# Experts' stage of an attention + capacity-routed MoE kernel: issue order of four engines from a booked model, six-round searches and lists on full 128x128 matmuls, W2 fetched apart from W1

## The chip, the core and the metric

The kernel runs on one core of a Trainium2 chip. The metric is the device time of one execution in microseconds. TensorE (PE in the profile) does the matmuls, VectorE (DVE) and ScalarE (ACT) the element-wise work, GpSimd (POOL) issues the gathers and scatters by index, SyncE (SP) issues the plain DMAs. Each engine works through its own queue in order; a semaphore holds an instruction until its operands are there, and everything behind it on that engine then waits too.

## What is computed

Two layers. The first is attention over 8 batches, 8 heads, 576 positions, with a local mask for four heads and a strided mask for the others. Its output, 4608 tokens of width 512, goes through eight experts, each with a capacity of 576 tokens:

```python
logits = x @ w_gate                      # x: [4608, 512], E = 8 experts
for idx in argsort(-logits.flatten()):   # greedy, best pair first
    tok, e = idx // E, idx % E
    if assigned[tok] >= 0 or counts[e] >= 576: continue
    assigned[tok] = e; counts[e] += 1
for e in range(E):
    h = maximum(x[assigned == e] @ w1[e], 0)     # 512 -> 1024
    out[assigned == e] = h @ w2[e]               # 1024 -> 512
```

## The kernel before

The change leaves the attention and the first expert's routing search (`search0`, L869) alone. What it rewrites is the stage of the eight experts, which begins where that search ends.

The greedy assignment is done expert by expert. An expert is "closed" at the score at which its 576th token is taken. `search` (L916) finds that score for the expert that fills next, on all 4608 tokens, 128 x 36, in `R1` = 7 rounds that each try `J1` = 17 thresholds: DVE compares every token with every threshold (L925), nine matmuls count the hits for four token columns at a time (L941, 68 output rows), DVE masks and sums them (L944, L947), one matmul folds the four column groups (L950), DVE compares with the capacity (L957), one matmul adds up over thresholds (L960), and DVE forms the next thresholds (L963). `number` (L981) then yields the expert's number; `weights` (L1079) reads it into a register of SP and issues eight DMAs of 512 KB for W1 and W2 (L1088); `slots` (L993) numbers the expert's tokens with a prefix sum (matmuls at L1010); `indices` (L1038) turns the slots into a token list with 36 matmuls of 32 output columns (L1064) and two that pick (L1072). `tokens` (L1167) gathers the rows with indirect DMAs on POOL (L1173) and turns them with transposing DMAs on SP (L1176; the first two or three tiles of expert 0 by PE, L1161).

Every weight matrix is split in a high and a low half-precision part: four squares on ACT (L1103) give a scale (a matmul at L1111), and eight cuts follow, each a scaled copy on ACT (L1121) and a difference on DVE (L1122). The f32 landing places of W1 and W2 exist once each, the split parts twice.

`ffn` (L1270) is the expert itself. Its first half, `hidden` (L1251), is 192 matmuls of W1 against the tokens (L1260) in eight groups; ACT (L1267) and DVE (L1268) take each group out of PSUM. Its second half is 96 matmuls of 512 columns (L1308) and 24 that run in pairs on 64 rows (L1302); ACT scales the result (L1318) and POOL scatters it (L1319).

The main loop (L1346 to L1365) walks through `ffn` and keeps a clock of PE's matmuls. The chains of the side work (search, slots, indices, weights) are generators that say after each step how long they sleep: fixed times such as `T_COUNT` = 2950, `T_SUM` = 1350, `T_STEP` = 1225 ns in a round and `T_PREFIX`, `T_HOT`, `T_LOAD` further on. Between two matmuls every chain that is due is advanced. `manual_schedule(engines=MAN)` makes the order written that way binding for PE alone (for ACT too in expert 0); the order on DVE, ACT, SP and POOL is the tile scheduler's, steered by `urgent()` (L837), which lifts the priority of a block. The chain of the next expert, in `side` (L1223), may not number an expert before the expert two ahead of it has been emitted (L1229).

Of the kernel before, what the change touches and what calls it, by code (L numbers as in the profile page):

```python
# [37 lines left out]
J1, R1, GC = 17, 7, 4  # L38
J0, JL, R0, CUTS0 = 32, 16, 6, (16, 12, 8)
TP = 128  # L40
# [5 lines left out]
URGENT = 4000  # L46
T_FIRST, T_COUNT, T_SUM, T_STEP, T_PREFIX, T_NEXT, T_HOT, T_DUP, T_LOAD = 1100, 2950, 1350, 1225, 3900, 2300, 4200, 550, 8000
PACE1 = 0.55
H0 = 256
HURRY = (0, 1, 7)  # L50
MAN, MAN0, MANP = {mybir.EngineType.PE}, {mybir.EngineType.Activation}, (0,)
T_W20, T_STEP0 = 9000, 1000
X1 = 100
SCALE_AT, TURN_AT, TAKE_AT, SEARCH_AT, TURN_U, W_EARLY, WARM0, WARM1, TURNS, TURN_E = 7, 9, 9, 10, 0, 1, 6, 4, 3, 2
T_F, T_LOAD0, T_HOT1, T_W, T_SQ, T_SCALE, T_CUT, T_BULK0 = 3000, 1500, 6350, 4000, 1500, 1500, 1500, 600
CUT0 = 1
EDGE0, PEAKS, PEAKS_N = 18, (24, 29), (1, 3)
LATE_Q, STORE_Q = (2, 3), ()
V_BITS, W1_BITS, W2_BITS = 8, 7, 15


def _constants():
# [31 lines left out]
    c["fold"] = np.concatenate([q[:, None] // J1 == x[None, :] // E, q[:, None] % J1 == np.arange(J1)[None, :]],  # L94
# [25 lines left out]
    pick = np.zeros((128, 2, 2, NT), np.float16)  # L120
    for g in range(4):
        for h in range(SHI):
            for a in range(3):
                for u in range(2):
                    for t in range(NT):
                        pick[32 * g + 3 * h + a, u, a // 2, t] = h == min(2 * t + u, SHI - 1)
    c["pick"] = pick.reshape(128, 4 * NT)
    c["iota"] = np.broadcast_to(np.arange(SLO, dtype=np.float16)[None, :, None], (TP, SLO, NC)).reshape(TP, SLO * NC)
# [4 lines left out]
def band_stride_attention_then_capacity_moe(ctx, tc, qt, kl, ks, nl, ns, wg, w1, w2, cst, out, dbg=None):  # L133
# [18 lines left out]
    fold = const.tile([GC * J1, GC * E + J1], F16, name="fold")  # L152
# [3 lines left out]
    pick = const.tile([128, 2, 2 * NT], F16, name="pick")  # L156
    iota = const.tile([TP, SLO, NC], F16, name="iota")
# [4 lines left out]
    nc.vector.memset(ones_j, 1.0)  # L162

    def late_constants():
        for t, name in ((desc8h, "desc_h"), (fold, "fold"), (small, "small"), (tri, "tri"), (pick, "pick"), (iota, "iota")):
            split_of = {"iota": NC, "pick": 2 * NT}.get(name)
            nc.sync.dma_start(t, cst[name].rearrange("q (s c) -> q s c", c=split_of) if split_of else cst[name])
        nc.sync.dma_start(val[:, :2], cst["val"].rearrange("q (a c) -> q a c", a=2))
# [667 lines left out]
    HV = 32  # L836
    rvb = [r1.tile([TP, HV, NC], F16, name=f"rv{i}") for i in range(2)]  # L837
    for t in rvb:
        nc.gpsimd.memset(t[:, 3 * SHI:], 0.0)
# [5 lines left out]
    def urgent(ph=1):  # L845
        return tc.high_priority(offset=URGENT * (2 if ph == 0 else 1))

    def spread(ph, todo):
        for step, f in todo:
            if ph not in rush:  # L850
                yield step if ph else min(step, T_BULK0)
            f()

    def slowly(todo):
        for step, f in todo:
            yield min(step, T_STEP0) if step != T_W20 else step
            f()
# [56 lines left out]
    def pace(t):  # L914
        return t if len(closed) > 1 else t * PACE1

    def search(rm, ohc, more):
        cand, src, top = cand0, rm, None
        ohv = ohc.rearrange("p c e -> p (c e)")
        for rd in range(R1):  # L920
            last = rd == R1 - 1
            t = cand[:, :J1] if last else cand[:, 1:J1 + 1]
            with urgent():
                cm = rt.tile([TP, NC, J1], F16, name="cm")
                nc.vector.tensor_tensor(cm, src[:, :, None].to_broadcast([TP, NC, J1]),  # L925
                                        t[:, None, :].to_broadcast([TP, NC, J1]), op=OP.is_ge)
                cv = cm.rearrange("p c j -> p (c j)")
                n = 1 if rd == R1 - 2 else J1 + 1
                if not last:
                    pre = cand[:, 0:1]  # L930
                    if n > 1:
                        pre = rt.tile([128, n], F32, name="pre1")
                        nc.vector.tensor_scalar(pre, steps[:, rd + 1, :n], cand[:, 0:1], None, op0=OP.add)
                if rd == 0:
                    more()
            yield pace(T_COUNT) + (X1 if len(closed) == 1 else T_FIRST if rd == 0 else 0)
            with urgent():
                pr = ps_r.tile([128, 512], F32, name="pr_")
                pc, p2, pm = pr[:GC * J1, :GC * E], pr[:J1, 64:64 + E], pr[:, 128:128 + (E if last else 1)]
                for k in range(0, NC, GC):  # L940
                    nc.tensor.matmul(pc, cv[:, k * J1:(k + GC) * J1], ohv[:, k * E:(k + GC) * E], start=(k == 0),  # L941
                                     stop=(k == NC - GC))
                red = rt.tile([GC * J1, GC, E], F16, name="red")
                nc.vector.tensor_tensor(red.rearrange("p c e -> p (c e)"), pc, fold[:, :GC * E], op=OP.mult)  # L944
                r8 = rt.tile([GC * J1, E], F16, name="r8")
                with nc.allow_low_precision(reason="whole numbers up to 1152"):
                    nc.vector.tensor_reduce(r8, red.rearrange("p c e -> p e c"), axis=AX.X, op=OP.add)  # L947
            yield pace(T_SUM)
            with urgent():
                nc.tensor.matmul(p2, fold[:, GC * E:], r8, start=True, stop=True, skip_group_check=True)  # L950
                g = rt.tile([J1, E], F16, name="g1")
                ih = rt.tile([J1, 1], F16, name="ih1")
                if last:
                    nc.vector.tensor_scalar(g, p2, float(CAP), None, op0=OP.is_ge)
                else:
                    with nc.allow_low_precision(reason="zero or one"):
                        nc.vector.tensor_scalar(g, p2, float(CAP), 0.0, op0=OP.is_ge, op1=OP.max, accum_out=ih)  # L957
            yield pace(T_STEP)
            with urgent():
                nc.tensor.matmul(pm, ones_j[:J1], g if last else ih, start=True, stop=True, skip_group_check=True)  # L960
                if not last:
                    cand = rt.tile([128, n], F32, name=f"cand{n}")
                    nc.vector.scalar_tensor_tensor(cand, steps[:, rd, J1 + 1:].to_broadcast([128, n]), pm, pre,  # L963
                                                   op0=OP.mult, op1=OP.add)
                if rd == R1 - 2:
                    top, src = cand, rt.tile([TP, NC], F32, name="rml")
                    nc.vector.tensor_scalar(src, rm, top, None, op0=OP.subtract)
                    cand = steps[:, rd + 1, :J1 + 1]
        with urgent():
            return settle(pm, top, steps[:, R1 - 1, J1 + 1:])  # L970
# [20 lines left out]
    def slots(ph, rm, ohc, wmc, code, mv):  # L991
        sc = rt.tile([TP, 2, NC], F16, name="sc")
        scf = sc.rearrange("p a c -> p (a c)")  # L993
        with urgent(ph):
            if mv is not None:
                mine = rt.tile([TP, NC], F16, name="mine")
                nc.vector.tensor_scalar(mine, wmc, code, None, op0=OP.is_equal)
                df = rt.tile([TP, NC], F32, name="df")
                nc.vector.tensor_scalar(df, rm, mv, None, op0=OP.subtract)
                nc.vector.scalar_tensor_tensor(sc[:, 0], df, steps[:TP, R1 - 1, J1 + 1:], mine, op0=OP.is_ge, op1=OP.mult)  # L1000
                nc.vector.scalar_tensor_tensor(sc[:, 1], df, 0.0, mine, op0=OP.is_ge, op1=OP.mult)
                nc.vector.tensor_tensor(sc[:, 1], sc[:, 1], sc[:, 0], op=OP.subtract)
            else:
                nc.vector.tensor_scalar(sc[:, 0], rm, -0.5 * BIG, None, op0=OP.is_ge)
                nc.vector.memset(sc[:, 1], 0.0)
        yield T_PREFIX
        with urgent(ph):
            pp = ps_r.tile([128, 512], F32, name="pr_")
            for j in range(2):
                nc.tensor.matmul(pp[:TP, j * 2 * NC:(j + 1) * 2 * NC], tri[:, j * TP:(j + 1) * TP], scf,  # L1010
                                 start=(j == 0), stop=(j == 1), skip_group_check=True)
            off = rt.tile([TP, 2 * NC], F32, name="off")
            nc.vector.tensor_scalar(off, scf, -8192.0, 8192.0, op0=OP.mult, op1=OP.add)
# [65 lines left out]
    def weights(ph, ei):  # L1079
        e = nc.sync.value_load(ei[0:1, 0:1], min_val=0, max_val=E - 1)  # L1080
        res, todo = [], []
        for name, w, nch, width, bits in (("w1", w1, DC, FF, W1_BITS), ("w2", w2, FC, DM, W2_BITS)):
# [3 lines left out]
            def fetch_w(cs, wf=wf, src=src, n4=n4):  # L1086
                for c in cs:
                    nc.sync.dma_start(wf[:, c * n4:c * n4 + n4], src[:, c * n4:c * n4 + n4])  # L1088
# [343 lines left out]
```

## Time and profile before

| | us |
|---|---|
| median of 3 runs | 702.52 (701.30 to 702.54) |
| the profiled execution, its own time | 707.31 |
| its span, first to last instruction | 705.5 |
| PE busy, DVE busy, ACT busy in the span | 613.3, 459.1, 360.9 |
| experts' stage, first to last of its main matmuls | 245.2 to 695.8 |

The profiled execution is 4.8 us above the median. Busy time of PE is modelled and overlapping matmuls count once, so a stage is read from the starts of the matmuls and from what PE waited for, not from the busy share.

### The profile page before, as it was taken

What the parts mean: (1) busy time and instruction counts of PE and PEld (TensorE: products, weight loads), DVE (VectorE), ACT (ScalarE), POOL (GpSimd) and SP (SyncE); (2) the same over time, 40 slices, a digit from 0 to 9 for tenths busy, and PEclk for the clock granted to TensorE, in tenths of its full rate; (3) what the DMA queues carried; (4) which work ended last, traced back from release to release, by engine and by line L of the source; (5) the groups of instructions that cost most, each with busy time, mean ns of one, the idle gap of its engine ahead of it and who ended that gap; (6) DMA issues with size and microseconds to landing.
All of it is one profiled execution on the core that took longest, in us unless ns stands there. A gap on an engine that the chain in (4) does not pass through costs nothing.

```text
span 705.5 us, 18314 instructions
## 1 busy us (share of the span) xinstructions
PE 613.3 (87%) x7519; PEld 398.8 (57%) x7519; DVE 459.1 (65%) x1377; ACT 360.9 (51%) x551; POOL 150.4 (21%) x166
## 2 busy tenths in 40 slices
PE   7686889888944599999999979998999998799994
PEld 3565667666733375457457437646645745455741
DVE  6678888888657779775775755766667563652210
ACT  7376778787420554761751643374185274743210
POOL 2041433143330300410320240050041032202011
PEclk9789999999775599999999998999999999899998
DMA  9987786874130740950860790392194089531001
GB/s 233 285 235 209 226 234 197 243 204 146 37 101 2 227 103 20 302 120 1 294 148 1 276 165 1 108 278 56 44 291 107 2 291 268 189 82 53 1 24 45
DMA packets 75776, 103.15 MB, mean 146 GB/s; under 512 B 43060, under 2 KB 52828, under 8 KB 75180
## 3 DMA queue, kind: packets, MB, share of 16 engines
q1 hardware_dynamic: 68892, 82.48, 40.8%
q0 software_dynamic: 6080, 19.10, 9.2%
q8 instruction: 59, 0.97, 0.6%
q10 hardware_dynamic: 720, 0.39, 0.2%
q14 instruction: 25, 0.20, 0.1%
HBM read 73.84 MB, written 18.87 MB: 131 GB/s over the span
## 4 chain that ended last, share of the span: by engine, by line
PE 20%; DMA 16%; issue 13%; DVE 6%; SPq 5%; POOL 2%; ACT 2%; POOLq 0%; DVEq 0%; ACTq 0%
PE ph L1260 18%; DMA w<-in_w_dram 9%; DMA xg<-x_scr,idx 5%; SPq L1176 3%; DMA xt<-xg 3%; DVE w2l L1122 2%; SPq L1088 2%; POOL out_dram L1319 1%; POOL xg L1173 1%; ACT jk L1103 1%; DVE hl L1268 1%; PE ph L1161 0%; ACT yl L1315 0%; DVE L L1029 0%; PE ph L1206 0%
## 5 line engine op out<-in xcount | busy, mean ns | idle before, releaser
L1260 PE MATMUL ph<-xt,w1h 128*128 128x288 f16 (+2 forms) x1024 | 183.1, 291 | 12.0 <-DMA xt<-xg 10.8
L1260 PEld LDWEIGHTS <-w1h 128*128 128x128 f16 x1024 | 97.9, 99 | 41.4 <-issue 7.7
L1319 POOL DMA_INDIRECT out_dram<-y,idx x40 | 43.2, 1081 | 351.2 <-ACT y L1318 325.1
L1260 PE MATMUL ph<-xt,w1l 128*128 128x288 f16 (+2 forms) x512 | 114.9, 292 | 0.0
L1267 ACT ACTIVATE hh<-ph 128x576 f16<-128x576 f32 (+2 forms) x72 | 42.8, 594 | 128.8 <-PE ph L1260 128.6
L1103 ACT ACTIVATE jk<-w 128x1024 f16<-128x1024 f32 x64 | 67.4, 1053 | 74.9 <-DMA w<-in_w_dram 73.9
L1308 PE MATMUL ph<-w2h,hl 128*128 128x512 f16 x256 | 97.2, 380 | 0.0
L1308 PE MATMUL ph<-w2l,hh 128*128 128x512 f16 x256 | 97.2, 380 | 0.0
L1308 PE MATMUL ph<-w2h,hh 128*128 128x512 f16 x256 | 97.2, 380 | 0.0
L1308 PEld LDWEIGHTS <-hh 128*128 128x128 f16 x512 | 48.4, 98 | 54.5 <-issue 5.3
L1268 DVE SCALAR_TENSOR_TENSOR hl<-ph,hh 128x576 f16<-128x576 f32 (+2 forms) x72 | 49.5, 687 | 44.5 <-ACT hh L1267 44.3
L1260 PEld LDWEIGHTS <-w1l 128*128 128x128 f16 x512 | 50.3, 99 | 13.2 <-issue 0.6
L1173 POOL DMA_INDIRECT xg<-x_scr,idx x40 | 41.7, 1041 | 50.1 <-issue 34.1
L1318 ACT ACTIVATE y<-ph,so 128x512 f32<-128x512 f32 x32 | 21.8, 682 | 58.3 <-PE ph L1308 41.0
L1122 DVE SCALAR_TENSOR_TENSOR w1l<-w,w_sw,w1h 128x512 f16<-128x512 f32 x64 | 45.6, 744 | 9.1 <-ACT w1h L1121 9.0
L1122 DVE SCALAR_TENSOR_TENSOR w2l<-w,w_sw,w2h 128x512 f16<-128x512 f32 x64 | 45.7, 742 | 8.1 <-ACT w2h L1121 7.9
L465 POOL TENSOR_TENSOR xos<-xs,xos 118x384 f16<-118x384 f32 x32 | 31.8, 1020 | 70.1 <-ACT xos L463 70.1
L1121 ACT ACTIVATE w2h<-w,w_sw 128x512 f16<-128x512 f32 x64 | 41.1, 710 | 4.8 <-DVE w_sw L208 4.8
L1121 ACT ACTIVATE w1h<-w,w_sw 128x512 f16<-128x512 f32 x64 | 41.7, 708 | 3.3 <-DVE w_sw L208 2.1
L1308 PEld LDWEIGHTS <-hl 128*128 128x128 f16 x256 | 25.0, 97 | 27.3 <-issue 2.0
L465 POOL TENSOR_TENSOR xol<-xl,xol 128x256 f16<-128x256 f32 (+1 forms) x32 | 25.2, 808 | 69.0 <-ACT xol L463 62.7
L410 ACT ACTIVATE pr<-spa 128x576 f32<-128x576 f32 x32 | 20.8, 649 | 35.7 <-PE spa L407 31.2
(633 smaller groups left out, 1001.8 us busy)
## 6 DMA issues: line engine op xcount, KB each, us to landing
w<-in_w_dram SPq DMA_DIRECT2D x64, 512.0 KB
kl<-in_kl_dram SPq DMA_DIRECT2D x8, 608.0 KB
v_s<-in_ns_dram SPq DMA_DIRECT2D x16, 292.5 KB
v_l<-in_nl_dram SPq DMA_DIRECT2D x16, 292.5 KB
ql<-in_qt_dram SPq DMA_DIRECT2D x8, 576.0 KB
ks<-in_ks_dram SPq DMA_DIRECT2D x7, 576.0 KB
qs<-in_qt_dram SPq DMA_DIRECT2D x7, 576.0 KB
x_scr<-xol SPq DMA_DIRECT2D x28, 128.0 KB
```

The source lines that it names most:

```text
L465: eng.tensor_tensor(u.xo[:nr, t, 1, c], xf[:, t], u.xo[:nr, t, 0, c], op=OP.subtract)
L1103: nc.scalar.activation(jk, wf[:, c * n4:(c + 1) * n4].rearrange("p c f -> p (c f)"), AF.Square, scale=1.41422, accum_out=sq[:, c:c + 1])
L1121: nc.scalar.activation(hi[:, c, f], wf[:, c, f], AF.Copy, scale=s_)
L1122: nc.vector.scalar_tensor_tensor(lo[:, c, f], wf[:, c, f], s_, hi[:, c, f], op0=OP.mult, op1=OP.subtract)
L1173: nc.gpsimd.indirect_dma_start(out=xg[:n], out_offset=None, in_=x_rows, in_offset=bass.IndirectOffsetOnAxis(ap=idx[:n, t:t + 1], axis=0))
L1176: nc.sync.dma_start_transpose(xt[:, :, t * 128:t * 128 + n], xg[:n])
L1260: nc.tensor.matmul(tile_[:, j, :w], wt[:, d, f * 128:(f + 1) * 128], xt[:, d // 2, xx, d % 2, c], start=(k == 0), stop=(k == 3 * DC - 1))
L1267: nc.scalar.activation(hv, src, AF.Relu)
L1268: nc.vector.scalar_tensor_tensor(lv, src, 0.0, hv, op0=OP.max, op1=OP.subtract)
L1308: nc.tensor.matmul(py, a[:, f, ts_], w[:, f], start=(k == 0), stop=(k == len(todo) - 1))
L1318: nc.scalar.activation(y, py, AF.Copy, scale=so[:, t:t + 1])
L1319: st = nc.gpsimd.indirect_dma_start(out=out_rows, out_offset=bass.IndirectOffsetOnAxis(ap=idx[:n, t:t + 1], axis=0), in_=y[:n], in_offset= ...
```

## The change

The constants of the search become `J1, R1 = 32, 6`: 32 thresholds in six rounds. All matmuls of the side work get 128 x 128 weights: the count gives 4 x 32 = 128 rows, the fold matrix is 128 x 128, the last sum uses 128 rows of `ones_q`; the list is made by 18 matmuls, each for two token columns, and the picking by eight. The sleeping times, `urgent` and the pacing are dropped. In their place `spend(engine, cost, ready)` books each instruction of ACT, DVE and POOL on a clock of that engine, PE's own side matmuls are added to the clock, and a chain sleeps until the booked end of what it waits for plus a `GAP` of 200 ns; `poll` runs due chains from a heap, then cuts and squares when ACT is booked free, then the low halves when DVE is. The order so found is binding for PE, ACT, DVE and SP. A class `Weights` fetches W1 when the expert is numbered and the old W1 has been cut, and W2 in a job of its own that waits until all 16 cuts of the old expert are out. `ensure` forces cuts that PE needs next. W2's first square comes before the cuts of W1, in expert 0 too.

The diff, cut to its core:

```diff
-J1, R1, GC = 17, 7, 4
+J1, R1, GC = 32, 6, 4
-MAN, MAN0, MANP = {mybir.EngineType.PE}, {mybir.EngineType.Activation}, (0,)
+MAN = {mybir.EngineType.PE, mybir.EngineType.Activation, mybir.EngineType.DVE, mybir.EngineType.SP}
+GAP, PE_LAG, LAND0, LAND_N, XG_LAG = 200, 150, 3500, 1600, 6000
+C_COUNT, C_SMALL, C_LIST, C_TURN = 290, 75, 800, 560
...
+    def spend(eng, cost, ready=0.0):
+        free[eng] = max(clock, free[eng], ready) + cost
+        return free[eng]
...
+    def poll():
+        while events and events[0][0] <= clock:
+            _, n, j = heapq.heappop(events)
+            if j.n == n:
+                j.step()
+        more = True
+        while more and free[ACT_] <= clock:
+            more = False
+            for w in splits:
+                if w.ready() <= clock:
+                    w.step()
+                    more = True
+                    break
+            splits[:] = [w for w in splits if w.todo]
+        while lows and free[DVE_] <= clock and lows[0][0] <= clock:
+            low()
...
     def search(rm, ohc, more):
...
+            due = spend(DVE_, 1330) + GAP
...
-            yield pace(T_COUNT) + (X1 if len(closed) == 1 else T_FIRST if rd == 0 else 0)
-            with urgent():
-                pr = ps_r.tile([128, 512], F32, name="pr_")
-                pc, p2, pm = pr[:GC * J1, :GC * E], pr[:J1, 64:64 + E], pr[:, 128:128 + (E if last else 1)]
+            yield due
+            pc = ps_r.tile([128, 512], F32, name="pr_")[:, :GC * E]
...
-            yield pace(T_SUM)
+            yield spend(DVE_, 440, clock + PE_LAG) + GAP
+            p2 = ps_r.tile([128, 512], F32, name="pr_")[:, :E]
+            nc.tensor.matmul(p2, fold[:, GC * E:], r8, start=True, stop=True)
+            pe(C_SMALL)
...
+            yield spend(DVE_, 250, clock + PE_LAG) + GAP
+            pm = ps_r.tile([128, 512], F32, name="pr_")[:, :E if last else 1]
+            nc.tensor.matmul(pm, ones_q, g if last else ih, start=True, stop=True)
...
     def indices(ph, slot):
...
-            for c in range(NC):
-                g = c % 4
-                nc.tensor.matmul(pi[HV * g:HV * g + HV, :SLO], rv[:, :, c], ohl[c // nh][:, :, c % nh], start=(c < 4),
-                                 stop=(c >= NC - 4), skip_group_check=True)
+        for k in range(NC // 2):
+            both = ohl[k // nh][:, k % nh].rearrange("p s u -> p (s u)")
+            nc.tensor.matmul(pi[:, :6 * SH2], both, rv[:, :, 2 * k:2 * k + 2], start=(k == 0), stop=(k == NC // 2 - 1))
+        pe(C_LIST)
...
+    class Weights:
+        def __init__(w, ph, ei):
+            w.ph = ph
+            w.e = nc.sync.value_load(ei[0:1, 0:1], min_val=0, max_val=E - 1)
+            w.todo = [("sq", 1, k) for k in range(4)] + [("scale", 1, 0), ("sq", 2, 0)] + [("cut", 1, k) for k in range(8)] + \
+                [("sq", 2, k) for k in range(1, 4)] + [("scale", 2, 0)] + [("cut", 2, k) for k in range(8)]
...
+        def ensure(w, i, k):
+            need = k + 1 if i == 1 else 9 + k
+            while w.cut < need:
+                while w.todo and w.cut + sum(x[1] is w for x in lows) < need:
+                    w.step()
+                while lows and w.cut < need:
+                    low()
...
     def side(src, more):
...
             while ph >= 2 and ph - 2 not in emitted:
-                yield None
-            with urgent():
-                oh, ei, code = number(w8)
-            wts = weights(ph, ei)
+                yield clock + 400
+            old = work[ph - 1][0]
+            oh, ei, code = number(w8)
+            spend(DVE_, 450)
+            w = Weights(ph, ei)
+            old.ensure(1, 7)
+            w.fetch(1)
+            splits.append(w)
+            Job(load2(w, old), clock)
...
+            while ph not in listed:
+                yield clock + 100
             if ph < E - 1:
...
-                yield T_NEXT
+                yield spend(DVE_, 3000)
...
+    def load2(w, old):
+        while not old.done():
+            yield clock + 400
+        w.fetch(2)
...
     def hidden(w, xt, hh, hl, f, js):
...
+        w.ensure(1, f)
...
+        def leave():
...
             nc.scalar.activation(hv, src, AF.Relu)
+            yield spend(ACT_, 60 + n * wd) + 60
             nc.vector.scalar_tensor_tensor(lv, src, 0.0, hv, op0=OP.max, op1=OP.subtract)
+            spend(DVE_, 80 + n * wd * 1.1)
...
     with tc.manual_schedule(engines=MAN):
...
         for ph in range(E):
+            while ph not in work:
+                wait(clock + 200)
+            wait(work[ph][4])
+            for cost in ffn(ph, *work[ph][:4]):
+                clock += cost
+                poll()
+            emitted.add(ph)
```

## Rows read from the trace of the kernel before

**Rows 1.** Busy us by stretch (PE, PEld, DVE, ACT, POOL, clock, DMA): last expert; all eight.

```profile
648.60:695.80 47.20, 47.20 (x313) 29.21 (x311) 6.81 (x9) 8.64 (x13) 4.79 (x5) 1.00 0.08 26
sum 450.60, PE 428.37 PEld 259.75 DVE 269.35 ACT 212.04 POOL 78.65; mean PE 53.55 PEld 32.47 DVE 33.67 ACT 26.51 POOL 9.83
```

**Rows 2.** Timeline of PE in a search round (start, us, line, tiles, shape, count).

```profile
358.24 0.38 PE L1308 MATMUL ph<-w2h,hh 128*128 128x512 f16 x1
358.46 0.45 PE L941 MATMUL pr__5780<-ohn,cm 128*68 128x32 f16 x9
358.75 0.38 PE L1308 MATMUL ph<-w2l,hh 128*128 128x512 f16 x1
...
360.04 0.38 PE L1308 MATMUL ph<-w2l,hh 128*128 128x512 f16 x1
360.35 0.18 PE L950 MATMUL pr__5780<-r,fold 68*17 68x8 f16 x1
360.46 0.39 PE L1308 MATMUL ph<-w2h,hl 128*128 128x512 f16 x1
...
361.55 0.38 PE L1308 MATMUL ph<-w2l,hh 128*128 128x512 f16 x1
361.86 0.17 PE L960 MATMUL pr__5780<-ih,ones_j 17*128 17x1 f16 x1
361.96 0.39 PE L1308 MATMUL ph<-w2h,hl 128*128 128x512 f16 x1
362.19 0.17 PE L1111 MATMUL pr__5832<-ss,ones_b 128*128 128x1 bf16 x1
362.22 0.28 PE L1260 MATMUL ph<-xt,w1h 128*128 128x288 f16 x1
```

**Rows 3.** Timeline of PE at the making of a token list.

```profile
574.13 1.30 PE L1064 MATMUL pr__8597<-ohl,rv 128*32 128x64 f16 x36
575.37 0.39 PE L1308 MATMUL ph<-w2h,hl 128*128 128x512 f16 x1
```

**Rows 4.** Waits of PE from 245 to 697 (waiter, releaser: total us, times, longest).

```profile
PE ph L1260 <- DMA xt<-xg: 10.8, 8, 2.5
PE pr__8935 L1064 <- DVE rv L1050: 5.2, 1, 5.2
...
PE pr__4891 L1072 <- DVE p L1067: 1.1, 1, 1.1
...
PE pr__7218 L950 <- DVE r L947: 0.2, 1, 0.2
```

**Rows 5.** Busy us by stretch: sum of 420.5 to 427.3 and 604.8 to 611.6.

```profile
sum 13.60, PE 10.42 PEld 6.56 DVE 4.23 ACT 4.01 POOL 1.11; mean PE 5.21 PEld 3.28 DVE 2.11 ACT 2.01 POOL 0.56
```

**Rows 6.** Busy us by stretch: first half of expert 1, second half of expert 1.

```profile
307.40:334.90 27.50, 26.53 (x238) 20.01 (x237) 19.19 (x60) 10.24 (x16) 0.96 (x1) 1.00 0.05 14
334.90:362.20 27.30, 27.30 (x197) 12.79 (x196) 18.95 (x64) 17.26 (x29) 9.83 (x9) 1.00 0.93 275
```

**Rows 7.** Timeline of PE: four small matmuls with full-width weights, at half clock.

```profile
203.86 0.27 PE L565 MATMUL spare<-wgh,xtd 128*128 128x16 f16 x4 [0.23 <-DMA xtd<-x_scr]
```

**Rows 8.** Line L565's weight loads (ns min/median/max, first and last start).

```profile
L565 PEld LDWEIGHTS <-xtd x20: 103/105/129, 203.9 to 205.1; 128*128 128x128 f16 x16, 128*64 128x64 f16 x4
```

**Rows 9.** DVE's compares by shape, 205 to 245 (busy us, mean ns).

```profile
L879 DVE TENSOR_TENSOR cm<-rm,nx 128x512 f16<-128x512 f32 x4 | 2.8, 691 | 0.1
L879 DVE TENSOR_TENSOR cm<-rm,nx 128x384 f16<-128x384 f32 x4 | 2.2, 551 | 0.0
...
L925 DVE TENSOR_TENSOR cm<-rmn,cand 128x612 f16<-128x612 f32 x1 | 0.8, 795 | 0.0
```

**Rows 10.** Timeline of ACT at the start of expert 0.

```profile
241.45 1.95 ACT L1121 ACTIVATE w1h<-w,w_sw 128x512 f16<-128x512 f32 x3 [1.24 <-PE pr__4156 L1111]
244.12 1.02 ACT L1163 ACTIVATE xt<-ph 128x1024 f16<-128x1024 f16 x1 [0.72 <-PE ph L1161]
```

**Rows 11.** The page's costliest groups: a square (xcount, busy us, mean ns).

```profile
L1103 ACT ACTIVATE jk<-w 128x1024 f16<-128x1024 f32 x64 | 67.4, 1053 | 74.9 <-DMA w<-in_w_dram 73.9
```

More of the change, by code (lines that the diff above doesn't have):

```diff
@@ L1 @@
-from contextlib import ExitStack, nullcontext
+import heapq
+from contextlib import ExitStack
+from itertools import count
 import numpy as np
@@ L958, in search @@
[L958 to L968, printed above, removed]
@@ new lines, in search @@
+            if rd == 0:
+                more()
+                spend(DVE_, 450)
+            yield due
+            pc = ps_r.tile([128, 512], F32, name="pr_")[:, :GC * E]
+            for k in range(0, NC, GC):
+                nc.tensor.matmul(pc, cv[:, k * J1:(k + GC) * J1], ohv[:, k * E:(k + GC) * E], start=(k == 0),
+                                 stop=(k == NC - GC))
+            pe(C_COUNT)
+            red = rt.tile([128, GC, E], F16, name="red")
+            nc.vector.tensor_tensor(red.rearrange("p c e -> p (c e)"), pc, fold[:, :GC * E], op=OP.mult)
@@ L972, in rest @@
+        spend(DVE_, 700, clock + PE_LAG)
+        return settle(pm, top, steps[:, R1 - 1, J1 + 1:])
     def rest():
@@ new lines, in slots @@
+        due = spend(DVE_, 950 if mv is not None else 350) + GAP
+        off = rt.tile([TP, 2 * NC], F32, name="off")
+        nc.vector.tensor_scalar(off, scf, -8192.0, 8192.0, op0=OP.mult, op1=OP.add)
+        spend(DVE_, 200)
+        yield due
+        pp = ps_r.tile([128, 512], F32, name="pr_")
+        for j in range(2):
+            nc.tensor.matmul(pp[:TP, j * 2 * NC:(j + 1) * 2 * NC], tri[:, j * TP:(j + 1) * TP], scf,
+                             start=(j == 0), stop=(j == 1), skip_group_check=True)
@@ L1322, in ffn @@
-            for s in scat:
-                tc.declare_no_dep(st.ins, s.ins, reason="rows of other tokens")
-            scat.append(st)
-    clock, chains = 0, []
-    with tc.manual_schedule():
-        src0, now = first_round()
-    def load0():
-        ready.add(0)
-        yield 0
-    def due_now():
-        return clock
-    def advance(c):
-        try:
-            step = next(c[1])
-        except StopIteration:
-            chains.remove(c)
-            return
-        c[0] = max(c[0], clock) + (300 if step is None else step)
@@ new lines, in ffn @@
+                for k, (a, b, f) in enumerate(seq):
+                    if t == 0 and k % 3 == 0:
+                        w.ensure(2, f)
+                        for j in jobs if f == 0 and ph == 0 else [jobs[f]]:
+                            if j is not jobs[-1] or f == FC - 1:
+                                force(j)
+                    nc.tensor.matmul(py, a[:, f, ts_], b[:, f], start=(k == 0), stop=(k == len(seq) - 1))
+                    yield 216
+            leaving.append(Job(leave(t, py), clock + PE_LAG))
```

613 lines of the change are left out of this document (310 added, 303 removed).

## The prediction

> **What bounds the kernel now.** I read four views, in this order.
>
> First the busy time by stretch, to see what an expert costs when nothing disturbs it. The last expert has no side work beside it, and takes 47.2 us at a granted clock of 1.00 [rows 1]. Eight such would be 377.6 us. The eight experts take 450.6 [rows 1]. So 73.0 us of the stage are not the experts' own matmuls, and only these can be won. DVE is busy for 269 us and ACT for 212 of the 450.6 [rows 1]: neither is full.
>
> Second the timeline of PE, to see what the side work takes from it. A main matmul of 512 columns starts 0.22 us after the one before. Where a count of nine matmuls stands between, the next starts after 0.51, so the count costs 0.30; the fold costs 0.42 less 0.22, 0.20; the last sum 0.41 less 0.22, 0.20 too [rows 2]. A round is 0.70, and 42 rounds are 29.4 us. The 36 matmuls of a list hold the next main one up by 1.24 [rows 3]; seven lists are 8.7. Against that a single full-width matmul of the scale holds it up by 0.03 only (362.22 less 361.96, less 0.22) [rows 2].
>
> Third what PE waited for: 10.8 us for turned tokens at the heads of the experts, 5.2 for the list of the last expert, and twelve smaller waits for DVE from 1.1 down to 0.2, together 6.1 [rows 4]: 22.1.
>
> Fourth the clock. In two stretches after such waits PE ran at half of its clock, 1.2 GHz, and was busy for 10.4 us in them [rows 5]; half of that, 5.2, was lost. The start of expert 0 is at half clock too; it stays so.
>
> These make 65.4 of the 73.0; the start at half clock, prefixes, scales, picks and PE's turning are the rest.
>
> Why PE waits at the heads: during the first half of expert 1 the DMA engines are 5% busy, during its second half 93% [rows 6]. The next expert is numbered only when the first half ends, and weights, list, gather and turning must fit into the 27.3 us of the second half. They just miss.
>
> **The change, part by part.**
>
> *Full-width matmuls, six rounds.* Four matmuls with 128 columns of weights took 0.27 us together with 0.17 for the last to end, so they start about 0.03 apart, and that at half clock [rows 7]; the lone scale matmul cost 0.03 [rows 2]. A new round is then nine counts and two sums at 0.03: 0.33. 36 rounds are 11.9 us: 17.5 less. A list is 18 at 0.03, 0.54; its 60 columns of 2.4 GHz take 0.025, under that. Seven are 3.8: 4.9 less; the diff itself books 0.8 for one, which would make it 3.1 less. Eight picks at 0.03 replace two narrow matmuls: counted at nothing, 0.1 either way each.
>
> From the other side: if the loads of 128-column weights did not overlap one another, each would cost its 0.10 [rows 8]. I take 0.03, which both the lone and the repeated matmul show [rows 2, 7].
>
> *DVE.* A compare grows from 612 to 1152 elements. From 384 to 512 elements the time rises from 0.55 to 0.69 [rows 9], 1.1 ns an element, so 1152 take 1.39. 36 at 1.39 less 42 at 0.80 [rows 9] is +16.5 us, less some of the small operations of six saved rounds. That lies on DVE: 269 and 16 of about 412 us, some 70%. It is hidden as long as search and splits finish within an expert; without that cover it is the first rival below.
>
> *The order and the earlier chain.* The sleeps go, so the search runs as fast as its engines hand over: per round a compare of 1.4, three small steps of DVE and three trips to PE. Today one round goes from its first count to its last sum in 3.4 us [rows 2] with the compare not yet in it. Six rounds of 4 to 6 are 24 to 36 us. Then the next expert can be numbered at the head of an expert's first half, not at its end, and the chain that now has 27 us gets about 50. The waits at the heads, 10.8, go, and the 5.2 of the last list; with them the half-clock stretches that followed, 5.2. What is late next is PE's own stream.
>
> Moved with it: W1's four DMAs and W2's four go out on SP right after the number, with the transposes of the same expert behind them. The transposes wait for gathers on SP, and a W2 that had to come later would stand behind them; in the steady state the old cuts are out before and it does not. On POOL the gathers now stand among the scatters of the running expert, each behind a result that ACT writes; with 20 us to spare that is counted at nothing. If that spare time is gone, it is the first rival again.
>
> *The small waits.* PE's order is fixed, so a count placed before its compare is done stops the main matmuls too. Today about 160 handovers cost 6.1 us, 0.04 each. There will be about 145 (36 rounds of three, lists, scales), placed closer to their operands, behind a DVE that also works in a fixed order: a cut there waits for ACT, ACT for a landing, and the count behind the cut for all of them. Not in the trace. Lower bound 2 us; upper bound one operation of about 0.7 us, the size of a compare of 512 elements [rows 9], ahead of every second handover, 50 us. I take 0.06 each, 9 us, near to today's rows [rows 4], since the diff books 1.33 for the compare that I make 1.39, and adds a gap of 0.2. That is 2.9 more.
>
> *The start.* Today W1's first cut is out at 241.45 on, before ACT copies the turned tokens at 244.12 [rows 10]. In the new order W2's first square (1.05 [rows 11]) and the first cut (0.65, three in 1.95 [rows 10]) come behind that copy, and the first matmul needs them: 1.7 later. The chain before it is otherwise the same; list and tables there change by some tenths either way, counted at nothing.
>
> **Sum.** 17.5 + 4.9 + 10.8 + 5.2 + 5.2 - 2.9 - 1.7 = 39.0 us less. The profiled execution took 707.3 (span 705.5), so it would take 668. The runs' median is 702.5, 4.8 lower, and I can't see where: if it is in the waits and half-clock stretches, they have less to give. Taken from the median the sum is 663.5; taking half of the 4.8 from the gain, 666. I forecast 666.
>
> **The rivals.**
>
> *The head start doesn't come.* DVE is so full that rounds take 6 to 7 us and the next expert is numbered late as now. For: DVE's 16 us more, strict order. Against: it was idle for 180 of 450 us [rows 1]. Then the waits (10.8, 5.2) and half-clock stretches (5.2) mostly stay, some 17 of 21: 683. This is also what happens if the booked order does nothing and only the shapes count.
>
> *Slower: PE stops at handovers.* One mechanism, at L941, L950, L960 and the scales' matmuls: PE reaches them before DVE does. Each costs the delay of whatever DVE has queued in front. From 0.06 + 36.5/145 = 0.31 us each on average the gain is gone; that is less than half of an operation of 0.7. At 0.4 the time is 666 + 145 x 0.34 = 715. For: today's chains are spaced by sleeps of 1.2 to 3 us and even so twelve of them waited. Against: those that waited were few.
>
> *Full-width weights load one after another.* Each count then costs 0.10 [rows 8]: a round 0.97, a list 1.87, 23.0 and 9.3 us more than I took: 698. The Trainium skill, "TensorE: Matmul & The Clock Gate", section "Back-to-back issue gap", says of streams of weight load and matmul that with 128 columns one comes every 81 ns or so; by its figure a round would be 0.79 and the time, as an estimate, about 689. The rows speak against both: 0.03 apart with full weights, at half clock [rows 7].
>
> *Better:* hardly any waits, and the whole gain from the median: below 657.
>
> **How the numbers follow.** Forecast as summed, within 657 to 678: 0.66. Head start missing, 678 to 692: 0.12. Slower by handovers: 0.10. Weights in line: 0.04. Better: 0.04. Between the first and the second rivals, the same within 0.2%, about what a measurement of this kernel can tell from no change: 0.04. Faster is 0.66 + 0.12 + 0.04 + 0.04 = 0.86, the same 0.04, slower 0.10. The range from 652 to 692 holds the forecast, the missing head start and nearly all of the better case, and leaves 0.18 to 0.2 out; it takes in the bounds of the list and of the waits up to 0.25 each.
>
> **What would show it.** Right: main matmuls 0.25 apart at a fold or sum, 0.5 at a count; DMA busy during first halves; no row of turned tokens among PE's long waits; a clock of 1.00 from 255 on; experts of 49 to 52 us. The start is right if the first main matmul starts near 247. Wrong: many rows of PE waiting for `cm`, `r`, `g` or `ss` of DVE that add up to over 20 us; an expert's first matmul still ended by a transpose; fold and sum still at 0.2 each. The forecast fails if one order of DVE or ACT puts an instruction that waits for a landing ahead of what PE needs, in each expert anew.

## The result and the profile after

The change made the kernel slower by 0.7%: 708.17 us against 702.62 of before, medians of 20 runs each; the ratio is 1.0073 with an interval from 1.0045 to 1.0102. So it is slower beyond the noise, by less than 1%. The forecast was 666. The times of one kernel scatter by about a per cent and the chips differ too, so below every kernel is given by its ratio to runs of before on the same chip, with its interval; "us" after a ratio is that ratio times 702.6, and the expectations' times are read against it.

The profiled execution after took 709.14 us, its span is 707.4. Busy time by stretch of the kernel after (us of the stretch, PE, PEld, DVE, ACT, POOL, clock, DMA share, GB/s): first half of expert 0, its second half, the gap behind it, the halves of experts 1 to 5, and the last expert.

```profile
247.71:278.60 30.89, 27.45 (x256) 21.07 (x256) 21.62 (x61) 17.50 (x35) 0.00 (x0) 0.95 0.27 67
278.60:307.40 28.80, 26.38 (x173) 12.42 (x171) 21.82 (x69) 10.77 (x18) 5.85 (x6) 1.00 0.49 180
307.40:320.40 13.00, 1.46 (x23) 0.88 (x23) 7.66 (x21) 7.08 (x12) 5.69 (x4) 0.68 1.08 192
320.40:349.20 28.80, 28.05 (x255) 21.91 (x256) 23.38 (x71) 13.92 (x23) 0.00 (x0) 0.91 0.22 78
349.20:384.70 35.50, 28.84 (x168) 12.53 (x167) 20.57 (x53) 12.66 (x21) 9.55 (x9) 0.90 0.59 152
384.70:410.40 25.70, 25.70 (x255) 20.93 (x254) 23.67 (x77) 14.61 (x24) 2.91 (x3) 1.00 0.27 100
410.40:439.70 29.30, 25.79 (x177) 11.78 (x175) 19.82 (x51) 12.55 (x21) 7.90 (x7) 1.00 0.71 179
439.70:465.20 25.50, 25.47 (x244) 20.74 (x245) 22.79 (x74) 14.52 (x24) 6.09 (x6) 1.00 0.48 147
465.20:493.80 28.60, 25.60 (x167) 11.68 (x165) 20.64 (x53) 13.30 (x22) 4.08 (x4) 1.00 0.57 142
493.80:519.50 25.70, 25.70 (x254) 20.92 (x253) 22.32 (x68) 13.86 (x24) 6.71 (x6) 1.00 0.70 166
519.50:547.40 27.90, 25.01 (x159) 11.31 (x156) 19.54 (x54) 13.12 (x22) 4.04 (x4) 1.00 0.41 127
547.40:572.90 25.50, 25.12 (x223) 20.21 (x222) 20.22 (x59) 13.96 (x24) 6.33 (x6) 1.00 0.63 161
572.90:602.00 29.10, 25.35 (x123) 10.95 (x122) 14.11 (x31) 17.88 (x29) 4.94 (x4) 0.94 0.45 126
...
650.40:697.70 47.30, 47.25 (x313) 29.25 (x311) 7.10 (x11) 8.65 (x14) 4.78 (x5) 1.00 0.08 26
sum 449.99, PE 411.56 PEld 257.33 DVE 288.66 ACT 211.62 POOL 78.89; mean PE 25.72 PEld 16.08 DVE 18.04 ACT 13.23 POOL 4.93
```

The stage takes 450.0 us, before 450.6 [rows 1], though PE is busy for 17 us less in it: what the smaller matmuls saved went into waits. (The profiled execution of before was one of its slow ones, 4.8 us above the median of its first three runs; so the 0.7% shows in the medians and not here.) The first halves of experts 2 to 5 are now 25.5 to 25.7 us, where that of expert 1 was 27.5 before [rows 6]; but their second halves are 27.9 to 29.3, where that of expert 1 was 27.3 before, and PE is idle for about 3 to 4 us in each. Between experts 0 and 1 there is a hole of 13.0 us, in and behind which the granted clock is below 1.00 (0.68, 0.91), and expert 1's second half takes 35.5.

What PE waited for from 245 to 700, after (in us: total, times, longest):

```profile
PE ph L1418 <- DVE w2l L1185: 13.4, 13, 1.9
PE ph L1337 <- DMA xt<-xg: 7.5, 2, 6.7
PE pr__5671 L998 <- DVE g L995: 4.0, 1, 4.0
PE pr__8560 L1194 <- DVE ss L1191: 3.7, 1, 3.7
PE ph L1337 <- DVE w1l L1185: 3.4, 4, 1.2
```

All rows of this view, of which the five longest stand here, add up to 39.4. The same view of before [rows 4] adds up to 23.2: the 22.1 of the prediction and 1.1 for ACT's copy of the first tokens, which it left out. The list of the last expert is not among them any more, and the turned tokens fell from 10.8 to 7.5. In their place stands a wait that before did not have at all: the second half for the low halves of its own W2.

What the new matmuls cost shows in PE's timeline after, in an undisturbed stretch (start, us, line, tiles, shape, count):

```profile
401.80 1.24 PE L1115 MATMUL pr__6108<-rv,ohl 128*128 128x60 f16 x18
402.86 0.31 PE L1337 MATMUL ph<-xt,w1h 128*128 128x288 f16 x1
...
407.25 0.38 PE L977 MATMUL pr__6188<-ohn,cm 128*128 128x32 f16 x9
407.48 0.53 PE L1337 MATMUL ph<-xt,w1h 128*128 128x288 f16 x3
...
409.47 0.17 PE L987 MATMUL pr__6243<-r,fold 128*128 128x8 f16 x1
409.49 0.28 PE L1337 MATMUL ph<-xt,w1l 128*128 128x288 f16 x1
```

From the start of each to the next main one: a count 0.23, a fold 0.02 to 0.03, a list 1.06.

**Where the low halves are.** Three pieces of the timelines after, expert 3 at 465.2 going into its second half: ACT with the high halves of its W2, DVE with the low halves, PE with its waits for them.

```profile
440.30 2.54 ACT L1184 ACTIVATE w2h<-w,w_sw 128x512 f16<-128x512 f32 x4
...
446.45 0.71 ACT L1184 ACTIVATE w2h<-w,w_sw 128x512 f16<-128x512 f32 x1
```

```profile
458.30 0.74 DVE L1185 SCALAR_TENSOR_TENSOR w2l<-w,w_sw,w2h 128x512 f16<-128x512 f32 x1
...
472.27 1.41 DVE L1185 SCALAR_TENSOR_TENSOR w2l<-w,w_sw,w2h 128x512 f16<-128x512 f32 x2
```

```profile
468.23 0.38 PE L1418 MATMUL ph<-w2l,hh 128*128 128x512 f16 x1 [1.35 <-DVE w2l L1185]
...
473.07 0.38 PE L1418 MATMUL ph<-w2l,hh 128*128 128x512 f16 x1 [0.70 <-DVE w2l L1185]
```

The last high half is out at 447.2, but the first low half starts at 458.3 and the last one ends at 473.7, over 8 us into the half that reads them. Expert 3 is no exception: in experts 1, 2 and 4 the last low half ends 9.7, 7.8 and 8.2 us into the second half; in expert 5 it is out 3.5 us before that half begins. `poll` lets a low half go only when DVE is booked free at that moment, and DVE's timeline has no idle time from 439.9 to 459: the next expert is numbered and listed then, and its tables and first compare are made.

**What a late low half does to the next expert.** Its W2 may go out only when all 16 cuts of the old expert are done. Timelines after, in the second half of expert 1: the last low halves of its own W2 on DVE, then SP, ACT, DVE and PE.

```profile
356.74 2.07 DVE L1185 SCALAR_TENSOR_TENSOR w2l<-w,w_sw,w2h 128x512 f16<-128x512 f32 x3
```

```profile
353.80 10.07 SPq L1231 DMA_TRANSPOSE xt<-xg  x5
364.14 2.11 SPq L1158 DMA_DIRECT2D w<-in_w_dram  x4
```

```profile
369.85 1.06 ACT L1173 ACTIVATE jk<-w 128x1024 f16<-128x1024 f32 x1 [6.53 <-DMA w<-in_w_dram]
...
370.91 2.54 ACT L1184 ACTIVATE w1h<-w,w_sw 128x512 f16<-128x512 f32 x4
```

```profile
371.65 0.75 DVE L1185 SCALAR_TENSOR_TENSOR w1l<-w,w_sw,w1h 128x512 f16<-128x512 f32 x1 [4.58 <-ACT w1h L1184]
372.31 0.16 DVE L995 TENSOR_SCALAR_CACHE_REDUCE g<-pr__5655 128x8 f16<-128x8 f32 x1
```

```profile
368.19 0.38 PE L1418 MATMUL ph<-w2l,hh 128*128 128x512 f16 x1
372.54 0.16 PE L998 MATMUL pr__5671<-ih,ones_q 128*128 128x1 f16 x1 [3.96 <-DVE g L995]
```

Read from top to bottom: the old cuts are out at 358.8, and not before could W2 go. On SP its four DMAs stand behind five transposes that wait for their gathers, and these end at 363.9: of the 10 us of transposes the last 5 hold W2 up (the first four of the eight DMAs in the SP row are W2 of this expert, the others W1 of the next). ACT waits for them at W2's first square, which the change puts ahead of W1's cuts; DVE stands at the low half of such a cut; the step `g` of the search stands behind that; PE stands at the last sum, and its main matmuls behind it. Whether the old low halves or the transposes end last differs from expert to expert: after the last old low half W2 goes 5.3, 2.5 and 7.6 us later in experts 2, 3 and 6, when the transposes end, and 0.1 us later in experts 4 and 5, where the transposes had ended and SP itself stood for the low halves. Waits of SP in the whole run:

```profile
SPq L1158 <- DVE w2l L1185: 8.0, 2, 5.4
```

### The profile page after: what moved, and what is told of

The parts are those of the page before. It is cut to its first block, busy times and chain, and to the rows that moved or that the text cites. A ratio compares the mean times of both kernels' runs of the same rounds, so it can differ in the third digit from the quotient of the medians.

```text
span 707.4 us, 17929 instructions
## 1 busy us (share of the span) xinstructions
PE 599.3 (85%) x7357; PEld 399.5 (56%) x7357; DVE 479.0 (68%) x1336; ACT 360.9 (51%) x551; POOL 150.2 (21%) x164
## 5 line engine op out<-in xcount | busy, mean ns | idle before, releaser
L1337 PE MATMUL ph<-xt,w1h 128*128 128x288 f16 (+2 forms) x1024 | 175.8, 288 | 8.7 <-DMA xt<-xg 7.5
L1337 PE MATMUL ph<-xt,w1l 128*128 128x288 f16 (+2 forms) x512 | 112.5, 289 | 3.4 <-DVE w1l L1185 3.4
L1418 PE MATMUL ph<-w2l,hh 128*128 128x512 f16 x256 | 98.8, 386 | 13.4 <-DVE w2l L1185 13.4
L1418 PE MATMUL ph<-w2h,hl 128*128 128x512 f16 x256 | 98.7, 386 | 0.0
L1391 POOL DMA_INDIRECT out_dram<-y,idx x40 | 41.3, 1033 | 260.0 <-ACT y L1389 233.3
L1227 POOL DMA_INDIRECT xg<-x_scr,idx x40 | 43.5, 1088 | 139.9 <-DVE idx L1128 64.6
L960 DVE TENSOR_TENSOR cm<-rmn,cand 128x1152 f16<-128x1152 f32 x30 | 40.8, 1358 | 0.9
```

Of the source, the lines that this page charges most:

```text
L1227: nc.gpsimd.indirect_dma_start(out=xg[:n], out_offset=None, in_=x_rows, in_offset=bass.IndirectOffsetOnAxis(ap=idx[:n, t:t + 1], axis=0))
L1337: nc.tensor.matmul(tile_[:, j, :wd], wt[:, d, f * 128:(f + 1) * 128], xt[:, d // 2, xx, d % 2, c], start=(k == 0), stop=(k == 3 * DC - 1))
L1391: st = nc.gpsimd.indirect_dma_start(out=out_rows, out_offset=bass.IndirectOffsetOnAxis(ap=idx[:n, t:t + 1], axis=0), in_=y[:n], in_offset= ...
L1418: nc.tensor.matmul(py, a[:, f, ts_], b[:, f], start=(k == 0), stop=(k == len(seq) - 1))
```

## The experiments

Each is the kernel after with the edit shown, except the first, which is the kernel before.

**Only the shapes.** The kernel before with six rounds of 32 thresholds and all full-width matmuls; its order and sleeping times stay, with `T_COUNT` 3540 for the longer compare.

```diff
-J1, R1, GC = 17, 7, 4
+J1, R1, GC = 32, 6, 4
```

> The kernel before with the new shapes alone: six rounds of 32 thresholds, full-width search, list and pick matmuls, the old sleeping times (only the sleep after the compare is 0.59 us longer, for the longer compare), the old order. If the shapes pay as in the trace of after (a round 0.29 us of PE against 0.70, a list 1.06 against 1.24 to 1.33), 42 x 0.70 less 36 x 0.29 is 19 us, so 683 to 688 against 702.6, and the new order then costs about 20 to 25 us by itself. If the shapes pay nothing in time (the chain of the next expert sets the end anyway), within 3 us of 702.6.

Measured: ratio 0.977 (0.967 to 0.988), 686.4 us. The time is in the range of the first expectation. The shapes alone bring some 16 us, so the new order costs about 21. The stage of this kernel is 427.9 us.

**W2 fetched with the number.** A second landing place for W2 (room for it from one `rv` buffer), and its DMAs right behind W1's.

```diff
-            w.wf[i] = wp.tile([128, nch, width], F32, name=name)
+            w.wf[i] = wp.tile([128, nch, width], F32, name=name, bufs=i)
...
-            Job(load2(w, old), clock)
+            w.fetch(2)
```

> After, with two landing places for W2, so that W2 is fetched right behind W1 and never waits for the old cuts or behind the transposes (the list's value tile has one buffer in place of two, for room). Theory A, a late W2 that the strict order of ACT and DVE hands on to PE: the waits at L998 (4.0), L1194 (3.7) and most of those for w2l (13.4) go, 690 to 695 against 708. Theory B, the low halves are booked last whatever arrives: the 13.4 stay, 700 to 704. The wait at the head of expert 1 (13 us) stays in both.

Measured: 0.983 (0.974 to 0.992), 690.4 us, 17 less than the change. The waits at L998 and L1194 are gone (the rows of 4.0 and 3.7), the low halves of W2 still hold PE up for 10.3 us, and expert 1 still starts 11.2 us late. So the time is that of theory A, while the waits for `w2l` stay as theory B had it.

**W1's cuts ahead of W2's first square.**

```diff
-            w.todo = [("sq", 1, k) for k in range(4)] + [("scale", 1, 0), ("sq", 2, 0)] + [("cut", 1, k) for k in range(8)] + \
-                [("sq", 2, k) for k in range(1, 4)] + [("scale", 2, 0)] + [("cut", 2, k) for k in range(8)]
+            w.todo = [("sq", 1, k) for k in range(4)] + [("scale", 1, 0)] + [("cut", 1, k) for k in range(8)] + \
+                [("sq", 2, k) for k in range(4)] + [("scale", 2, 0)] + [("cut", 2, k) for k in range(8)]
```

> After, with W2's first square behind the eight cuts of W1 in the list of work, nothing else. W1's cuts then no longer wait for W2's landing, and expert 0 starts 1 to 2 us earlier. Theory A: ACT no longer stands before a late landing with W1's cuts behind it, 4 to 8 us less: 700 to 704. Theory B: only the start, 706.

Measured: 1.002 (0.997 to 1.006), 703.7 us, some 4 less than the change, with intervals that overlap a little. That is the upper end of theory A's range, but not for its reason: expert 0 doesn't start earlier (248.1 against 247.7), and the late landing is still there, and PE meets it one step on, at the scale of W2. Two of its waits, from 243 to 720:

```profile
PE pr__8480 L1194 <- DVE ss L1191: 9.9, 1, 9.9
PE pr__5735 L1194 <- DVE ss L1191: 3.9, 1, 3.9
```

So what stands behind the landing decides little here; that W2 leaves late weighs more.

**Low halves let through earlier.**

```diff
-        while lows and free[DVE_] <= clock and lows[0][0] <= clock:
+        while lows and free[DVE_] <= clock + 1500 and lows[0][0] <= clock:
```

> After, with the low halves of the cuts booked on DVE as soon as DVE is booked free within 1.5 us, not only when it is free. Theory B, low halves starved behind search and drains: the 13.4 us of waits for w2l shrink to under 4, 695 to 699 against 708, and W2 of the next expert goes out earlier. Theory A: under 3 us.

Measured: 0.972 (0.963 to 0.982), 683.1 us, 25 less than the change, and more than either expectation had (theory B 9 to 13, theory A under 3). No wait for `w2l` is left, as theory B had it. With the cuts out in time, W2 goes right behind W1, ahead of the transposes, in every expert from 1 on; SP in this kernel, once:

```profile
388.83 5.34 SPq L1158 DMA_DIRECT2D w<-in_w_dram  x8
406.96 9.64 SPq L1231 DMA_TRANSPOSE xt<-xg  x5
```

What it leaves is the hole at the head of expert 1, from 300.6 to 314.6.

**Both of these.** 

> The changed kernel with two edits at once: a low half may be issued when DVE is booked up to 1.5 us ahead, and W2 has a second landing place and is fetched with the number. Alone they gave 684.0 and 689.9, 24 and 18 us under the changed kernel. One loop (late low halves make the next W2 late, its late landing makes the next low halves late): cutting it in two places gives little more than the better cut, 678 to 685, and PE waits for neither low halves nor squares. Two separate causes: the gains add, 666. In both, the 13 us stall at the head of expert 1 stays, since neither edit touches the search of expert 0.

Measured: 0.970 (0.961 to 0.980), 681.8 us. Alone the two brought 25 and 17, together 26. That is what one loop would give, and not two causes that add up: late low halves make W2 late, and a late W2 makes the next low halves late.

**DVE left to the scheduler.**

```diff
-MAN = {mybir.EngineType.PE, mybir.EngineType.Activation, mybir.EngineType.DVE, mybir.EngineType.SP}
+MAN = {mybir.EngineType.PE, mybir.EngineType.Activation, mybir.EngineType.SP}
```

> The changed kernel with the order of DVE left to the scheduler; PE, ACT and SP stay bound to the program order. Theory that DVE's strict order is the cause (low halves and steps of the search behind an instruction that waits): low halves are taken as soon as their high halves are out, 680 to 690, PE hardly waits for low halves. Theory that the place in the program is the cause (low halves are issued last, and a scheduler that goes by the program's order finds them just as late): within 1% of the changed kernel's 708, waits for low halves still over 8 us.

Measured: 1.030 (1.019 to 1.040), 723.5 us, outside both expectations. DVE and PE in this kernel, at the same late landing as above (SP gives W2 out at 362.47, behind transposes from 351.58):

```profile
370.09 2.08 DVE L1185 SCALAR_TENSOR_TENSOR w1l<-w,w_sw,w1h 128x512 f16<-128x512 f32 x3 [11.20 <-ACT w1h L1184]
372.08 0.18 DVE L981 TENSOR_TENSOR red<-pr__5634,fold 128x32 f16<-128x32 f32 x1
```

```profile
373.10 0.17 PE L987 MATMUL pr__5655<-r,fold 128*128 128x8 f16 x1 [11.07 <-DVE r L984]
```

The scheduler puts a low half that waits ahead of a step of the search, and PE stands for 11 us where it stood for 4. Taking the binding order from DVE does not mend the change, it costs another 16 us. Freeing ACT or SP was not tried.

**PE's lag in expert 0.** Low halves let through, and in expert 0 a main matmul counts 1.4 times on the booked clock.

```diff
-                clock += cost
+                clock += cost * (1.4 if ph == 0 else 1.0)
```

> The changed kernel with the low halves let through as before, and in expert 0 every main matmul counts 1.4 times on the booked clock, so that side matmuls stand after fewer main ones. With the low halves alone: 684.0, search from 244.7 to 284.5, head of expert 1 waiting 14.0 us. Theory of the lagging clock (PE comes to the count, fold and sum of expert 0 by 1 to 3 us after DVE is ready, because its own waits are not in the booked clock): 15 handovers each some 0.7 us sooner, the search ends about 10 us earlier, the head waits 4 to 6 us, 674 to 678. Theory of the full DVE (the chain stands behind cuts on DVE): the search ends within 2 us of 284.5, PE now waits at its small matmuls instead, 682 to 687. Theory of the transfers (the gathers and W2 share the DMA engines, which were busy at over 1.0 from 305 on): the search ends earlier but the head still waits over 10 us, 682 to 686.

Measured: 0.961 (0.954 to 0.968), 674.9 us, some 8 less than with the low halves alone, within the range of the lagging clock's theory. The third round of the search in expert 0, first DVE and PE with the low halves alone, then with this edit:

```profile
259.73 1.36 DVE L960 TENSOR_TENSOR cm<-rmn,cand 128x1152 f16<-128x1152 f32 x1
```

```profile
262.94 0.38 PE L977 MATMUL pr__4423<-ohn,cm 128*128 128x32 f16 x9
```

```profile
254.44 1.36 DVE L960 TENSOR_TENSOR cm<-rmn,cand 128x1152 f16<-128x1152 f32 x1
```

```profile
256.07 0.38 PE L977 MATMUL pr__4360<-ohn,cm 128*128 128x32 f16 x9
```

This count came 1.85 us after its compare had ended, now 0.27. It is the round that gained most: over all six the counts came 8.3 us after their compares, now 4.4, and from the first count to the sixth it takes 29.1 us instead of 37.8. So the search was not held by a full DVE, but by a PE that came late. PE's side matmuls stand after a fixed number of main ones, and in between PE waited for `w1l` (3.4 us in four places), which the booked clock knows nothing of. That is one source of the lag; the factor of 1.4 moves every handover of expert 0 forward, whatever its lag comes from, and what makes up the rest was not taken apart. The prefix of expert 1's tokens comes 33.8 us after the first main matmul (276.6 less 242.81) instead of 42.5 (287.1 less 244.63). The hole is gone, and part of expert 2's search fits into expert 0 as well. Busy time by stretch of this kernel, expert 0 and the other seven:

```profile
242.81:309.31 66.50, 58.13 (x473) 33.95 (x473) 59.97 (x174) 39.29 (x72) 11.00 (x9) 0.97 0.52 145
309.31:658.77 349.46, 347.83 (x2640) 220.59 (x2638) 226.26 (x622) 172.16 (x283) 70.54 (x65) 1.00 0.50 137
```

Up to expert 1's first matmul it takes 66.5 us, against 70.0 with the low halves alone and 72.7 in the change; the seven others take 349.5 us, against 357.9 and 377.3, and PE waits for 10.5 us in the whole stage.

**A larger gap at each handover.** Low halves let through, and `GAP` 600 instead of 200.

> The changed kernel with the low halves let through as before, and the gap between the booked end of an operand and its use raised from 200 to 600 ns. With the low halves alone: 684.0, some 10 us of PE's waits at counts, folds, sums and scales. Theory that PE stops at handovers (the forecast's slower rival): these waits go, up to 10 us less, 674 to 680. Theory that PE comes late to them as it is: each round 1.2 us longer, expert 0's search 6 to 7 us longer and the stall at the head of expert 1 with it, later heads still covered: 688 to 694.

Measured: 1.016 (1.005 to 1.027), 713.7 us, 31 more than with the low halves alone; in the direction of the second theory, at three times the upper end of its 4 to 10 us. PE's longest row of waits, from 246 to 700:

```profile
PE ph L1337 <- DMA xt<-xg: 24.5, 12, 7.3
```

Not only expert 0's search is longer: the heads of experts 2 to 6 are no longer covered either. What bounds this kernel is the chain of an expert, not the stops of PE at handovers.

**All three edits; the clock alone; a factor of 1.2.** The low halves, W2's second place and 1.4 together:

> The changed kernel with all three edits: low halves let through 1.5 us ahead, W2's second landing place with its fetch at the number, and 1.4 times the booked clock in expert 0. Low halves and clock alone gave 672.7, low halves and W2 679.9. One loop, cut once already: the W2 edit adds 0 to 4 us, 668 to 673. W2 as a cause of its own: another 10 or more, below 663.

Measured: 0.959 (0.950 to 0.968), 673.7 us (679.27 beside 708.69 of before on that chip), the same as without W2's place, as one loop would have it. The factor of 1.4 alone, on the change:

> The changed kernel with 1.4 times the booked clock in expert 0 alone; low halves as the change has them. The changed kernel took 708.2, with the low halves let through 684.0, with both 672.7. Independent causes: 11 us less than 708, 695 to 699, with the stall at the head of expert 1 under 6 us and the waits for low halves still over 8 us in the experts behind it. One common cause (the clock of expert 0 also sets when the cuts come out in all later experts): below 685. Low halves starve so that the earlier search can't be used: within 3 us of 708.

Measured: 702.89 beside 708.69 of before on that chip, 0.992 (0.988 to 0.996), 697.0 us, 11 less than the change; by the ratio, that is the figure of independent causes. Its trace bears this out in part only: expert 1 follows expert 0 without a hole, but 78.5 us after the start instead of 72.7, since PE now waits inside expert 0 (it is busy for 63.2 of the 78.5, at a mean granted clock of 0.89); the seven other experts take 369.7 us instead of 377.3; low halves of W2 still cost 9.6. While low halves starve, the earlier search is used in part. With all three edits and 1.2:

> As the kernel with all three edits, with 1.2 in place of 1.4. Theory of the lagging clock: PE's waits in expert 0 were some 9 of 67 us, a seventh, so 1.2 follows PE better than 1.4: fewer waits at counts, and the search still in time, 666 to 671. If the search was in time only because side matmuls run far ahead of the main ones, the head of expert 1 stalls again by 4 to 8 us: 672 to 677.

Measured: 0.964 (0.955 to 0.972), 677.0 us, which the runs can't tell from 1.4. The hole is 0.9 us. Neither expectation is met as a whole: the time is at the edge of the second's range, without its stall of 4 to 8 us. The right factor is not resolved.

The kernels with the low halves and the factor of 1.4 beat both the change and the kernel before, by 4% against the latter, and the shapes alone by 1.6% (0.961 to 0.977, on different chips, intervals just overlapping). The 4% were seen on two chips, 0.961 on one and 0.959, with W2's place, on another.

## Why the prediction was wrong

*Shapes: right.* 0.33 was forecast for a round, 0.23 and two of 0.03 are 0.29: 36 are 10.4 instead of 11.9. The list was mis-sized: 1.06 instead of 0.54, so seven save 1.3 us and not 4.9. In sum 19.0 and 1.3 are 20.3 of the forecast's 22.4, and the shapes alone measured 16 (9 to 23). Weights one after another, a rival, would have shown as 0.9 for a count. The 0.03 itself was in part luck: [rows 7] is the start of a longer run, which as a whole stands 0.07 apart at half clock ((1.48 - 0.17) / 19):

```profile
203.86 1.48 PE L565 MATMUL spare<-wgh,xtd 128*128 128x16 f16 x20 [0.23 <-DMA xtd<-x_scr]
```

Only the lone scale matmul [rows 2] showed 0.03, and it fits the counts (26 ns each), not the lists (59). The Trainium skill ("TensorE: Matmul & The Clock Gate", "Back-to-back issue gap") gives about 81 ns for each matmul of such a stream with 128 moving columns. The counts move 32 and the lists 60, so no run here shows that figure, and the rival's estimate of 689 took it to shapes that it is not given for.

*Head start: right in kind, late in coming.* The DMA share of first halves rises from 0.22 and 0.27 in experts 1 and 2 to 0.48, 0.70 and 0.63 in experts 3 to 5, against 0.05 [rows 6]; the waits of the heads behind expert 1 and of the last list are gone. But the chain begins in expert 0 without a head start, and there the rounds of 4 to 6 us were wrong: the change needs 35.5 us from its first count to its sixth (247.9 to 283.4), 7.1 a round. I counted how fast the engines hand over, not that PE meets a step only after a fixed number of main matmuls. A hole of 13.0 us came of it, with a granted clock of 0.68 in it and 0.91 and 0.90 in the halves behind it. The first rival had rounds of 6 to 7 us and a late number, but from a full DVE; the factor of 1.4 made the rounds shorter with a DVE that was busier (60.0 of 66.5 us in expert 0, with the low halves alone 51.5 of 70.0), so its reason was not the one.

*The cover that failed.* The step is this sentence: "a W2 that had to come later would stand behind them; in the steady state the old cuts are out before and it does not." They were not. The prediction treated the low halves as part of DVE's total, "hidden as long as search and splits finish within an expert", and that total did fit: DVE is busy for no more than 289 of 450 us. But its order matters, not its total: low halves are the last thing that `poll` issues, so in the expert shown they come after all of the next expert's numbering and listing, and in experts 1 to 4 the last is out 8 to 10 us into the half that reads them. That is worth 25 us, the largest cause that a single edit showed; the fetch of W2, 17 us by itself and 1 on top, is the same loop.

*Small waits: 9 us forecast, 39.4 found for all of PE's waits.* Of these 13.4 are for `w2l`, 3.4 for `w1l` and 7.5 for tokens. The counts, folds, sums and scales make some 14, or 0.1 each over 145 handovers, not the 0.31 of the slower rival, and a larger gap made the kernel slower still. That rival had the right sign and, for the most part, the wrong mechanism. The last sentence ahead of the forecast's line, a landing ahead of what PE needs, did happen, but twice (4.0 and 3.7, the second at the scale in expert 5, where ACT had waited 7.14 us for a W2 behind transposes), not in each expert. With low halves and clock mended all waits are 10.5 us, near to what was forecast.

*The start: wrong in its order, without weight.* ACT's first cuts of W1 still come before its copy of the turned tokens, and PE's first wait is for that copy (1.1). The 1.7 us can't be told from the scatter of the stage's start, 242.8 to 248.6 over the kernels.

*The sum.* With its two faults mended, the low halves and the booked clock of expert 0, the kernel takes 675 us by its ratio, within the forecast's 657 to 678. The order then brings some 11 us on top of the shapes (0.977 to 0.961), where the forecast had 16.6 (10.8 + 5.2 + 5.2 - 2.9 - 1.7). What is left of the difference is not taken apart.

## What to carry to other kernels

When a program fixes the order of every engine, look for the work that the issuing loop puts last and ask who waits for it; a mean load of 64% on its engine says nothing about when it gets its turn. A load that may only leave after that work has to be followed through the queue it shares: here it slid behind transposes that wait. A clock that books one engine must also count its stops, or what is placed by that clock comes later with each of them; here they were one part of a lag of which the rest stayed open.

## What the runs showed of the hardware beyond that

Eighteen matmuls of a list stand 59 ns apart (1.06 us), nine of a count 26 ns (0.23 us), though both load 128 x 128 weights each time. They differ in their moving columns, 60 taken in pairs at a stride against 32. A stride by itself does not do it: the eight matmuls that pick, with 10 or 5 columns at a stride, stand 27 ns apart (first at 406.06, last at 406.25). Whether it is the number of columns or both together was not tried.
